# A layernorm, gated feed-forward and Fourier-mixing kernel: a different reciprocal root and order of products in the opening, and a unit's four row tiles of the down product in one place

## The chip, the cores and the metric

The kernel runs on one core of a Trainium2 chip. The metric is the device time of one execution in microseconds (us). The kernel before took 769.42, 769.16 and 769.20 us in three runs, a median of 769.2. Engines: TensorE (PE, with its weight loads as PEld), VectorE (DVE), ScalarE (ACT), GpSimd (POOL) and SyncE (SP), which issues DMAs.

## The reference

```python
xn = layernorm(x)                      # x: 2048 rows of 448, eps 1e-5
a, b = xn @ dft_hid_re.T, xn @ dft_hid_im.T
s = dft_seq_re @ a - dft_seq_im @ b    # 2048 x 2048 by 2048 x 448
g = (gelu_tanh(xn @ w_gate) * (xn @ w_up)) @ w_down   # 448 -> 1792 -> 448
out = x + s * silu(g)
```

All of it is float32.

## The kernel before

**Precision.** Products run in a float32 format of the matrix unit that takes fewer bits than float32. Each operand is therefore kept as a high part and a low part (what the high part leaves), and a product is three: high by high, high by low, low by high. In the first products these are called "h0" or "hh" (high by high), "hl", and "lh" or "l0" (the low part of the weight); "last" is the last block of the contraction, which needs fewer. A high part is a copy by ScalarE, a low part a subtraction by VectorE or GpSimd.

**Stages.** The 2048 rows are 16 tiles of 128 in four chunks `c`, tile `k` of chunk `c` being `xr[c][:, k]`. The hidden dimension of 1792 is 14 blocks `f` of 128, in seven pairs, `GROUPS`. An opening normalizes and transposes chunk after chunk, and does the gate and up products of the first pair; groups 1 to 6 do those of the other pairs and the down products; the Fourier mixing follows, for the last 370 us, and is not touched.

**The opening.** SyncE loads tiles 0 and 1, the two raw weight blocks (`load_w`, `f` = 0 in two halves) and the other tiles. `stats` normalizes: `one` takes mean and variance on VectorE (`one.s` on ScalarE), `root` the square root on ScalarE, `newton` the reciprocal and one Newton step on VectorE, `norm` scales the tile. `turn_mm` transposes a tile on TensorE into a PSUM bank `pt`; ScalarE copies it out as the high part and VectorE subtracts for the low part (`turn_split`, in the first two tiles written out). `prep_w` splits the first weights by `high`, `low` and `rest`. `first(f, cols, parts)` issues products of the first chunk, for a half of its columns. `warm(n)` is n products on zeros, whose result nothing reads, put in where TensorE would stand.

**A unit.** Groups 1 to 6 have four units `bi` = 0 to 3, each one `f` and a pair `p` of chunks, done in `strassen` as seven sums of products in place of eight: 39 products of 512 columns, by `three` (L473) and `two` (L480), into four PSUM banks x1 to x4, which every unit uses again in that order. In a unit's second half: x1 is gelu'd by ScalarE into `g1` (L521), VectorE adds x3 to `u` into `c21` (L525) and multiplies `g1` by it (L526), ScalarE copies the high part of the hidden block `hs` out (L528) and VectorE subtracts for its low part (L530); VectorE adds x4 to `u` (L534) and ScalarE gelus it (L535). The other chunk's hidden block is finished in the next unit by `late` (L539, L541, L544).

**The down products.** A row tile of the down product is six products of 448 columns (`down_one`, L450) into a bank `po`; ScalarE copies it out (L457), and behind the fourth row tile of a chunk GpSimd issues a DMA (L462) that adds the chunk to `gs` in DRAM. They are kept in a list `dq` and issued one by one by `send` at places `dn[0]` to `dn[3]` of each unit: behind x2, behind x4's first half, behind x3 and at the end. `preps[0]` to `preps[3]` are four places for the splitting of the next weights (`prep_s`, L356 to L362, and `prep_d`, L384 and L385).

**What sets the order.** The program is scheduled by hand: each engine runs its instructions in the order in which the code issues them, and waits on semaphores for the others. `sums_s` issues ten additions or subtractions of 128 columns on GpSimd (L338 to L347), which make the sums of the next group's raw weights; it is called at the start of units `bi` = 1 and 2 in groups 2 to 5. `sum_step`, behind a unit, issues other DMAs, those that accumulate on GpSimd (L809). So in GpSimd's queue stand, in this order, the DMA of the down product of the unit that ends, in some units two DMAs of `sum_step`, and the sums.

Of the kernel before, what the change touches and what calls it, by code (L numbers as in the profile page):

```python
# [45 lines left out]
def fnet_geglu(ctx: ExitStack, tc: tile.TileContext, x, ca, ct, cp, et, wgu, wd, out):  # L46
# [45 lines left out]
    def tmp(i):  # L92
        return a_t[:, 512 * i : 512 * i + 512]
# [55 lines left out]
    def stats(c, k0, n):  # L149
        st = const.tile([P, 4, 6], F32, name=f"st{c}_{k0}", tag="st", bufs=2)  # L150
        mv = const.tile([P, 4, 2], F32, name=f"mv{c}_{k0}", tag="mv", bufs=3)
        sd = const.tile([P, 4, 4], F32, name=f"sd{c}_{k0}", tag="sd", bufs=3)

        def one(i):
            nc.vector.bn_stats(st[:, i], xr[c][:, k0 + i, :D])
            nc.vector.bn_aggr(mv[:, i], st[:, i])

        def one_s(i):

            xi, (mean, var), q = xr[c][:, k0 + i, :D], [mv[:, i, e : e + 1] for e in (0, 1)], sd[:, i, 2:3]  # L160
            nc.scalar.activation(tmp(0)[:, :D], xi, AF.Identity, accum_out=q)
            nc.scalar.activation(mean, q, AF.Copy, scale=1.0 / D)
            nc.scalar.activation(sd[:, i, 3:4], q, AF.Copy, scale=-1.0 / D)
            nc.scalar.activation(tmp(0)[:, :D], xi, AF.Square, bias=sd[:, i, 3:4], accum_out=q)
            nc.scalar.activation(var, q, AF.Copy, scale=1.0 / D)

        one.s = one_s

        def root():
            r, t, w = sd[:, :n, 0], sd[:, :n, 1], sd[:, :n, 2]  # L170
            nc.scalar.activation(t, mv[:, :n, 1], AF.Sqrt, bias=epst)
            nc.vector.tensor_scalar(w, mv[:, :n, 1], EPS, -0.5, op0=ALU.add, op1=ALU.mult)
            nc.vector.tensor_scalar_mul(sd[:, :n, 3], mv[:, :n, 0], -1.0)

        def newton():
            r, t, w = sd[:, :n, 0], sd[:, :n, 1], sd[:, :n, 2]
            nc.vector.reciprocal(r, t)

            nc.vector.tensor_mul(t, r, r)
            nc.vector.tensor_mul(t, t, w)  # L180
            nc.vector.scalar_tensor_tensor(r, t, 1.5, r, op0=ALU.add, op1=ALU.mult)

        def norm(i, eng=nc.vector):
            v = xr[c][:, k0 + i]
            if eng is nc.scalar:
                eng.activation(v, v, AF.Identity, bias=sd[:, i, 3:4])
                eng.activation(v, v, AF.Copy, scale=sd[:, i, 0:1])
            else:
                eng.tensor_scalar(
                    v, v, mv[:, i, 0:1], sd[:, i, 0:1], op0=ALU.subtract, op1=ALU.mult  # L190
                )

        return one, root, newton, norm
# [288 lines left out]
    def strassen(f, p, w, late, dn, preps):  # L482
# [42 lines left out]
        nc.vector.tensor_add(c21, u, x3)  # L525
# [20 lines left out]
        return late0, late1  # L546

    units_n = [0]


    with tc.manual_schedule():
# [15 lines left out]
        nc.scalar.activation(tbl, epst, AF.Sqrt)  # L567


        def warm(n):  # L570
            t = o_tile(f"warm{n}")
            for _ in range(n):
                nc.tensor.matmul(t, junk[:, :P], junk, start=True, stop=True)  # L573
# [5 lines left out]
        def first(f, cols, parts, gs=range(2)):  # L579

            for part in parts:
                if part == "h0":
                    for n, k in enumerate((1, 2, 0)):
                        for g in gs:
                            nc.tensor.matmul(  # L585
                                pgs[f][g][:, cols], block(ws[f], k, g)[0], xk(0, k)[:, cols],
                                start=n == 0, stop=False, skip_group_check=True,
                            )
                    continue
                for g in gs:  # L590
# [32 lines left out]
        nc.scalar.activation(xh[1], t1[2], AF.Copy)  # L623
        nc.vector.tensor_sub(xl[0], t0[2], xh[0])
        high0(None, 0, 512)
        low0(nc.gpsimd, 256, 512)
        rest0(nc.gpsimd)
        one, root, newton, norm = stats(0, 2, 2)
        nc.vector.tensor_sub(xl[1], t1[2], xh[1])
        one(0)  # L630
        high1(None, 512)
# [19 lines left out]
        turn_split(t2, t3, mid=lambda: one.s(3), ahead=lambda: (one(1), one(2), root()))  # L651
# [6 lines left out]
        first(1, half[1], ("lh",), (0,))  # L658
        t0, t1 = turn_mm(1, 0), turn_mm(1, 1)
        first(1, half[1], ("lh",), (1,))  # L660
        first(1, half[1], ("last",))
# [153 lines left out]
        def send():  # L815
            if dq:
                down_one(*dq.pop(0))

        nop = lambda: None

        e_at, e_raw = {}, {}

        def e_load(b):
# [19 lines left out]
        for gi in range(1, len(GROUPS)):  # L843
# [7 lines left out]
            for bi, (i, p) in enumerate(zip((0, 1, 1, 0), sides)):  # L851
# [55 lines left out]
                else:  # L907
# [501 lines left out]
```

## Time and profile before

| | us |
|---|---|
| median of three runs | 769.2 |
| the profiled execution, device time | 769.27 |
| its span in the profile | 767.5 |
| TensorE busy | 761.3 (99%) |
| VectorE busy | 544.4 (71%) |
| ScalarE busy | 366.6 (48%) |
| GpSimd busy | 179.9 (23%) |
| mean granted TensorE clock | 0.999 |

The page is of one execution. Its busy times say how full an engine is over the whole span; the chain that ended last says on which engine's work the end depends. A row of the timeline gives the start in us from the span's start, the length, engine, line and operation, the tiles written and read, and, in brackets, how long the engine had been idle and what ended that. A row with "x6" is six instructions in a row, and its length reaches from the first start to the last end. A row of the chain of waits gives start, length and what ran.

### The profile page before, as it was taken

The numbers are of one execution on the slowest core, as the hardware profiler recorded it, in microseconds if no ns is written. First come the engines' busy times: TensorE is split into PE (matmuls) and PEld (weight loads), VectorE is DVE, ScalarE is ACT, GpSimd is POOL, SyncE is SP. The second block draws the span as 40 slices with busy tenths as digits, with TensorE's granted clock in tenths as the row PEclk, the third lists the DMA queues.
The fourth block names the chain that finished last, engine by engine and source line by source line (L and its number), as shares of the span: only waits on it lengthen the run. The fifth ranks groups of instructions, "written<-read, shape, count | busy, mean of one in ns | idle before, by whom it ended". The sixth has DMA issues, their size and how long they took to land.

```text
span 767.5 us, 11360 instructions
## 1 busy us (share of the span) xinstructions
PE 761.3 (99%) x4054; PEld 686.2 (89%) x4054; DVE 544.4 (71%) x946; ACT 366.6 (48%) x547; POOL 179.9 (23%) x303
## 2 busy tenths in 40 slices
PE   8999999999999999999999999999999999999998
PEld 7988888888888888888889999999999999999997
DVE  7879877555556556455452777978888797979787
ACT  5975554444444344344444585534444444434341
POOL 2204043430501511501011001223222222323130
PEclk9999999999999999999999999999999999999999
DMA  8234458994959968774979981959696969688794
GB/s 298 91 120 150 145 203 172 263 186 104 266 107 252 272 117 225 172 157 84 257 218 240 372 346 54 325 170 334 210 354 205 346 202 343 211 304 268 256 312 153
DMA packets 61513, 170.04 MB, mean 222 GB/s; under 512 B 7440, under 2 KB 40080, under 8 KB 60560
## 3 DMA queue, kind: packets, MB, share of 16 engines
q0 software_dynamic: 13728, 61.02, 35.0%
q1 hardware_dynamic: 34272, 82.48, 30.5%
q10 hardware_dynamic: 13456, 25.81, 9.2%
q8 instruction: 32, 0.52, 0.3%
q14 instruction: 25, 0.20, 0.1%
HBM read 127.21 MB, written 70.91 MB: 258 GB/s over the span
## 4 chain that ended last, share of the span: by engine, by line
PE 99%; DVE 0%; issue 0%; DVEq 0%
PE x L473 24%; PE p L1173 22%; PE po L450 18%; PE p L1176 10%; PE ab L984 9%; PE x L480 4%; PE gu L396 4%; PE py L1188 1%; PE py L1190 1%; PE py L1189 1%; PE gu L599 1%; PE pt L198 1%; PE warm L573 1%; PE p L1206 0%; PE gu L585 0%
## 5 line engine op out<-in xcount | busy, mean ns | idle before, releaser
L473 PE MATMUL x<-xt,w 128*128 128x512 f32 x480 | 149.6, 392 | 0.0
L473 PEld LDWEIGHTS x<-xt,w 128*128 128x128 f32 x480 | 90.1, 188 | 16.3 <-DVE tmp L512 0.7
L457 ACT ACTIVATE po_out<-po 128x448 f32<-128x448 f32 x112 | 60.2, 537 | 81.7 <-PE po L450 79.5
L450 PE MATMUL po<-wd0h,hs 128*128 128x448 f32 x256 | 81.7, 366 | 0.0
L462 POOL DMA_DIRECT2D gs<-po_out x24 | 21.4, 893 | 218.7 <-ACT po_out L457 213.7
L984 PE MATMUL ab<-e,xt 128*128 128x448 f32 x288 | 68.8, 365 | 0.0
L450 PE MATMUL po<-wd,hs 128*128 128x448 f32 x288 | 66.0, 365 | 0.0
L473 PE MATMUL x<-t_v,w 128*128 128x512 f32 x216 | 60.8, 390 | 0.0
L450 PEld LDWEIGHTS po<-wd,hs 128*128 128x128 f32 x288 | 54.1, 188 | 6.7
L984 PEld LDWEIGHTS ab<-e,xt 128*128 128x128 f32 x288 | 54.1, 188 | 4.3
L450 PEld LDWEIGHTS po<-wd0h,hs 128*128 128x128 f32 x256 | 48.1, 188 | 4.9
L473 PEld LDWEIGHTS x<-t_v,w 128*128 128x128 f32 x216 | 40.6, 188 | 8.7
L1064 POOL DMA_DIRECT2D raw<-sums x45 | 24.8, 552 | 94.9 <-DVE xt L143 56.6
L450 PE MATMUL po<-wd0l,hs 128*128 128x448 f32 x128 | 46.9, 367 | 0.0
L142 ACT ACTIVATE e<-raw 128x896 fp32r<-128x896 f32 (+1 forms) x30 | 27.6, 921 | 38.6 <-DVE raw L1071 27.8
L528 ACT ACTIVATE hs<-tmp 128x512 fp32r<-128x512 f32 x24 | 15.2, 634 | 54.6 <-DVE tmp L526 54.6
L473 PE MATMUL x<-t_lo,w 128*128 128x512 f32 x96 | 37.4, 389 | 0.0
L142 ACT ACTIVATE e<-tmp 128x896 fp32r<-128x896 f32 (+1 forms) x22 | 19.7, 896 | 35.7 <-DVE tmp L1071 28.6
L1173 PE MATMUL p<-t_v,wd0l 128*128 128x448 f32 x112 | 36.4, 374 | 0.0
L1173 PE MATMUL p<-w,e 128*128 128x448 f32 x112 | 36.4, 374 | 0.0
L1064 POOL DMA_DIRECT2D tmp<-sums x39 | 21.5, 552 | 59.9 <-DVE xt L143 37.2
L358 DVE TENSOR_TENSOR w<-raw,w 128x512 fp32r<-128x512 f32 (+1 forms) x24 | 21.3, 888 | 18.3 <-ACT w L356 18.3
(374 smaller groups left out, 2017.6 us busy)
## 6 DMA issues: line engine op xcount, KB each, us to landing
gs<-po_out POOLq DMA_DIRECT2D x24, 896.0 KB, 7.8
sums<-ca SPq DMA_DIRECT2D x16, 896.0 KB, 11.2
sums<-ca POOLq DMA_DIRECT2D x16, 896.0 KB, 14.5
t_v<-td ACTq DMA_DIRECT2D x24, 448.0 KB, 5.8
w<-td ACTq DMA_DIRECT2D x24, 448.0 KB, 7.5
raw<-ct SPq DMA_DIRECT2D x45, 192.0 KB, 4.2
raw<-wgu SPq DMA_DIRECT2D x12, 640.0 KB, 5.9
tmp<-ct SPq DMA_DIRECT2D x39, 192.0 KB, 4.6
```

The source lines that it names most:

```text
L142: nc.scalar.activation(h, src, AF.Copy)
L358: nc.vector.tensor_sub(w[:, 1408 + lo : 1408 + b], raw[:, P + lo : P + b], hw[:, lo:b].bitcast(F32))
L396: nc.tensor.matmul(ps[:, cols], a, xt[:, cols], start=n == 0, stop=n == len(mm) - 1)
L450: nc.tensor.matmul(po[:, :D], hs[:, a, kk * P : (kk + 1) * P], wdn[b][:, i], start=n == 0, stop=n == 5,)
L457: nc.scalar.activation(out_[0][:, kk], po[:, :D], AF.Copy)
L462: nc.gpsimd.dma_start(gv[:, 4 * c : 4 * c + 4], out_[0], accum_op=ALU.add)
L473: nc.tensor.matmul(ps, a[i], b[j], start=first and n == 0, stop=n == 2, skip_group_check=True)
L480: nc.tensor.matmul(ps, a[0], xt, start=False, stop=True, skip_group_check=True)
L984: nc.tensor.matmul(p[:, :D], a, b, start=n == 0, stop=n == len(mm) - 1)
L1064: nc.gpsimd.dma_start(v[:, 4 * P : 6 * P], sums[j][:, KS.index(k)])
L1173: nc.tensor.matmul(ps[q][:, :D], h, v, start=u % UN == 0, stop=False, skip_group_check=True)
L1176: nc.tensor.matmul(ps[q][:, :HD], l, v[:, :HD], start=False, stop=u % UN == NS - 1, skip_group_check=True,)
```

## The change

In the opening, `root` becomes one ScalarE function that gives the reciprocal root at once; `newton` keeps the Newton step, in two operations per tile for a statistic of two tiles. Both halves of a weight's high part are copied by ScalarE (one of them was a VectorE cast), the low parts of the second weight go from GpSimd to VectorE, the two halves of the first weight's load change places, one product of `warm` goes, and the products of the first half-chunk are put in another order: both weights' high-by-high and the first weight's low-by-high come first. In groups 2 to 6, 17 of the 20 units issue their four row tiles together at `dn[1]`, in the middle, and the second step of the weight splitting ahead of them; group 1 and the last three units of group 6 keep their places.

```diff
         def root():
-            nc.scalar.activation(t, mv[:, :n, 1], AF.Sqrt, bias=epst)
-            nc.vector.tensor_scalar(w, mv[:, :n, 1], EPS, -0.5, op0=ALU.add, op1=ALU.mult)
-            nc.vector.tensor_scalar_mul(sd[:, :n, 3], mv[:, :n, 0], -1.0)
+            nc.scalar.activation(sd[:, :n, 0], mv[:, :n, 1], AF.Abs_reciprocal_sqrt, bias=epst)
         def newton():
-            nc.vector.reciprocal(r, t)
+            nc.vector.tensor_scalar(w, mv[:, :n, 1], EPS, -0.5, op0=ALU.add, op1=ALU.mult)
+            if n == 2:
...
+                for i in range(2):
+                    nc.vector.scalar_tensor_tensor(
+                        ti[i], ri[i], wi[i], ri[i], op0=ALU.mult, op1=ALU.mult
+                    )
+                for i in range(2):
+                    nc.vector.scalar_tensor_tensor(
+                        ri[i], ti[i], 1.5, ri[i], op0=ALU.add, op1=ALU.mult
+                    )
+                return
...
-        for b in (4, 0) if f == 0 else (None,):
+        for b in (0, 4) if f == 0 else (None,):
...
-        warm(4)
+        warm(3)
...
-        high0(nc.vector.tensor_copy, 512)
+        high0(None, 0, 512)
+        high0(None, 512)
         low0(nc.gpsimd, 512)
+        low0(nc.gpsimd, 256, 512)
+        rest0(nc.gpsimd)
...
         high1(None, 512)
-        one(1)
+        high1(None, 0, 512)
         root()
-        high1(None, 0, 512)
-        low1(nc.gpsimd, 256, 512)
-        rest1(nc.gpsimd)
...
         low1(nc.vector, 512)
+        low1(nc.vector, 256, 512)
+        rest1(nc.vector)
...
-        first(0, half[0], ("h0", "hl", "lh", "last"))
-        first(1, half[0], ("h0", "hl"))
+        first(0, half[0], ("h0", "l0"))
+        first(1, half[0], ("h0",))
+        first(0, half[0], ("hl", "last"))
+        first(1, half[0], ("hl",))
         t2, t3 = turn_mm(0, 2), turn_mm(0, 3)
-        first(1, half[0], ("lh", "last"))
+        first(1, half[0], ("l0", "last"))
...
         preps[1]()
+        if dn[0] is nop:
+            preps[2]()
         dn[1]()
...
-        preps[2]()
+        if dn[0] is not nop:
+            preps[2]()
...
-                dn = [send] * 4
-                if gi == 1 and bi < 2:
-                    dn = [nop, send, nop, send]
+                dn = [nop, lambda: [send() for _ in range(4)], nop, nop]
+                if gi == 1 or (bi and not nxt):
+                    dn = [send] * 4 if gi > 1 or bi > 1 else [lambda: None, send, nop, send]
```

ScalarE's first instructions before, from the first root on (`sd` holds the statistics, `pt` a transposed tile, `raw_74` and `raw_75` the two raw weights):

```order
L171 ACTIVATE sd_0_124<-mv_0_123,epst 128x2
L622 ACTIVATE xt_66<-pt_0_137 128x4x128
L623 ACTIVATE xt_66<-pt_1_143 128x4x128
L314 ACTIVATE w<-raw_74 128x512
L314 ACTIVATE wd_78<-raw_75 128x512
L171 ACTIVATE sd_2_163<-mv_2_162,epst 128x2
L314 ACTIVATE wd_78<-raw_75 128x512
```

The same place now:

```order
L174 ACTIVATE sd_0_124<-mv_0_123,epst 128x2
L326 ACTIVATE w<-raw_74 128x512 x2
L641 ACTIVATE xt_66<-pt_0_136 128x4x128
L642 ACTIVATE xt_66<-pt_1_142 128x4x128
L326 ACTIVATE wd_78<-raw_75 128x512 x2
L174 ACTIVATE sd_2_160<-mv_2_159,epst 128x2
```

The weight copies of the first weight stand ahead of the transposed tiles, and both of the second ahead of the second root.

VectorE before, from the first root on (`xr_a` holds the tiles of rows that are scaled):

```order
L172 TENSOR_SCALAR sd_0_124<-mv_0_123 128x2
L173 TENSOR_SCALAR sd_0_124<-mv_0_123 128x2
L177 RECIPROCAL sd_0_124<-sd_0_124 128x2
L179 TENSOR_TENSOR sd_0_124<-sd_0_124 128x2
L180 TENSOR_TENSOR sd_0_124<-sd_0_124 128x2
L181 SCALAR_TENSOR_TENSOR sd_0_124<-sd_0_124 128x2
L189 TENSOR_SCALAR xr_a<-xr_a,mv_0_123,sd_0_124 128x512 x2
L316 CAST w<-raw_74 128x512
```

The same place now:

```order
L178 TENSOR_SCALAR sd_0_124<-mv_0_123 128x2
L182 SCALAR_TENSOR_TENSOR sd_0_124<-sd_0_124 128x1 x2
L186 SCALAR_TENSOR_TENSOR sd_0_124<-sd_0_124 128x1 x2
L201 TENSOR_SCALAR xr_a<-xr_a,mv_0_123,sd_0_124 128x512 x2
L644 TENSOR_TENSOR xt_66<-pt_0_136,xt_66 128x4x128
L645 TENSOR_TENSOR xt_66<-pt_1_142,xt_66 128x4x128
```

Four steps on both tiles at once have become two steps for each tile, and the cast of the first weight is gone.

TensorE in the first unit of group 2 (`f` = 4, `p` = 1; the banks are x1 = `x_4_1_1225`, x2 = `x_4_1_1235`, x3 = `x_4_1_1252`, x4 = `x_4_1_1260`; `po_2_k` is row tile k of chunk 2), before, from the end of x2 on:

```order
L450 MATMUL po_2_0_1244<-wd_78,hs_80 128x448 x3
L450 MATMUL po_2_0_1244<-wd_78,hs_79 128x448 x3
L473 MATMUL x_4_1_1252<-xt_69,w 128x512
L473 MATMUL x_4_1_1252<-t_lo,w 128x512
L473 MATMUL x_4_1_1252<-xt_69,w 128x512
L473 MATMUL x_4_1_1252<-t_v_822,w 128x512 x3
L473 MATMUL x_4_1_1260<-xt_69,w 128x512
L473 MATMUL x_4_1_1260<-t_lo,w 128x512
L473 MATMUL x_4_1_1260<-xt_69,w 128x512
L473 MATMUL x_4_1_1260<-t_v_822,w 128x512 x3
L450 MATMUL po_2_1_1271<-wd_78,hs_80 128x448 x3
L450 MATMUL po_2_1_1271<-wd_78,hs_79 128x448 x3
```

Now, from x4's first half on (x4 is `x_4_1_1246`):

```order
L485 MATMUL x_4_1_1246<-xt_69,w 128x512
L485 MATMUL x_4_1_1246<-t_lo,w 128x512
L485 MATMUL x_4_1_1246<-xt_69,w 128x512
L485 MATMUL x_4_1_1246<-t_v_816,w 128x512 x3
L462 MATMUL po_2_0_1259<-wd_78,hs_80 128x448 x3
L462 MATMUL po_2_0_1259<-wd_78,hs_79 128x448 x3
L462 MATMUL po_2_1_1267<-wd_78,hs_80 128x448 x3
L462 MATMUL po_2_1_1267<-wd_78,hs_79 128x448 x3
L462 MATMUL po_2_2_1275<-wd_78,hs_80 128x448 x3
L462 MATMUL po_2_2_1275<-wd_78,hs_79 128x448 x3
L462 MATMUL po_2_3_1283<-wd_78,hs_80 128x448 x3
L462 MATMUL po_2_3_1283<-wd_78,hs_79 128x448 x3
```

The first row tile has moved behind x3 and x4, the third and fourth ahead of the rest of x1 and x3, so that the 24 products of the four stand in a row.

ScalarE in the second unit of group 2 (`f` = 5, `p` = 1), before: L500 copies x1, L541 is of the unit ahead.

```order
L500 ACTIVATE tmp<-x_5_1_1332 128x512
L541 ACTIVATE hs_79<-tmp 128x512
L457 ACTIVATE po_out<-po_3_0_1351 128x448
L457 ACTIVATE po_out<-po_3_1_1375 128x448
L521 ACTIVATE tmp<-x_5_1_1332 128x512
L528 ACTIVATE hs_79<-tmp 128x512
L457 ACTIVATE po_out<-po_3_2_1397 128x448
L535 ACTIVATE tmp<-tmp 128x512
L457 ACTIVATE po_out<-po_3_3_1413 128x448
```

Now:

```order
L512 ACTIVATE tmp<-x_5_1_1326 128x512
L556 ACTIVATE hs_79<-tmp 128x512
L469 ACTIVATE po_out<-po_3_0_1361 128x448
L469 ACTIVATE po_out<-po_3_1_1369 128x448
L469 ACTIVATE po_out<-po_3_2_1377 128x448
L469 ACTIVATE po_out<-po_3_3_1385 128x448
L535 ACTIVATE tmp<-x_5_1_1326 128x512
L543 ACTIVATE hs_79<-tmp 128x512
L550 ACTIVATE tmp<-tmp 128x512
```

All four copies of row tiles stand ahead of the gelu of x1 (L521, now L535), and so the fourth, behind which GpSimd's DMA goes, does. On GpSimd no instruction of a unit has changed its place in the queue.

More of the change, by code (lines that the diff above doesn't have):

```diff
@@ L548, in fnet_geglu @@
     units_n = [0]
+    nop = lambda: None
     with tc.manual_schedule():
@@ L566, in fnet_geglu @@
         tbl = const.tile([P, 1], F32, name="tbl")
-        nc.scalar.activation(tbl, epst, AF.Sqrt)
+        nc.scalar.activation(tbl, epst, AF.Abs_reciprocal_sqrt)
         def warm(n):
@@ L581, in first @@
             for part in parts:
-                if part == "h0":
+                if part in ("h0", "l0"):
                     for n, k in enumerate((1, 2, 0)):
@@ L585, in first @@
                             nc.tensor.matmul(
-                                pgs[f][g][:, cols], block(ws[f], k, g)[0], xk(0, k)[:, cols],
-                                start=n == 0, stop=False, skip_group_check=True,
+                                pgs[f][g][:, cols], block(ws[f], k, g)[part == "l0"], xk(0, k)[:, cols],
+                                start=part == "h0" and n == 0, stop=False, skip_group_check=True,
                             )
@@ L619, in fnet_geglu @@
         (high0, low0, rest0, _), (high1, low1, rest1, _) = ws
-        high0(nc.vector.tensor_copy, 512)
+        high0(None, 0, 512)
+        high0(None, 512)
         low0(nc.gpsimd, 512)
+        low0(nc.gpsimd, 256, 512)
+        rest0(nc.gpsimd)
         nc.scalar.activation(xh[0], t0[2], AF.Copy)
         nc.scalar.activation(xh[1], t1[2], AF.Copy)
+        one, root, newton, norm = stats(0, 2, 2)
         nc.vector.tensor_sub(xl[0], t0[2], xh[0])
[L625 to L628, printed above, removed]
         nc.vector.tensor_sub(xl[1], t1[2], xh[1])
         one(0)
+        one(1)
         high1(None, 512)
-        one(1)
+        high1(None, 0, 512)
         root()
-        high1(None, 0, 512)
-        low1(nc.gpsimd, 256, 512)
-        rest1(nc.gpsimd)
         for k, t in enumerate((t0, t1)):
@@ L642, in fnet_geglu @@
         low1(nc.vector, 512)
+        low1(nc.vector, 256, 512)
+        rest1(nc.vector)
         ws = [w[3] for w in ws]
         draw = load_d(GROUPS[0], a_r[0][:, 1024:])
-        first(0, half[0], ("h0", "hl", "lh", "last"))
-        first(1, half[0], ("h0", "hl"))
+        first(0, half[0], ("h0", "l0"))
+        first(1, half[0], ("h0",))
+        first(0, half[0], ("hl", "last"))
+        first(1, half[0], ("hl",))
         t2, t3 = turn_mm(0, 2), turn_mm(0, 3)
-        first(1, half[0], ("lh", "last"))
+        first(1, half[0], ("l0", "last"))
         one, root, newton, norm = stats(1, 0, 4)
         one(0)
-        turn_split(t2, t3, mid=lambda: one.s(3), ahead=lambda: (one(1), one(2), root()))
+        var3 = one.s(3)
+        one(1)
+        turn_split(t2, t3, mid=var3, ahead=lambda: (one(2), root()))
         newton()
@@ L657, in fnet_geglu @@
         first(1, half[1], ("hh", "hl"))
-        first(1, half[1], ("lh",), (0,))
         t0, t1 = turn_mm(1, 0), turn_mm(1, 1)
-        first(1, half[1], ("lh",), (1,))
-        first(1, half[1], ("last",))
+        first(1, half[1], ("lh", "last"))
         turn_split(t0, t1)
@@ L817, in send @@
                 down_one(*dq.pop(0))
-        nop = lambda: None
         e_at, e_raw = {}, {}
```

9 lines of the change are left out of this document (6 added, 3 removed).

## The prediction

> **What bounds the kernel now.** I read the page first, then the waits by engine, then the chain of waits in order of time, and last the timeline of the opening and of single units.
>
> The page's first and fourth parts, and the waits of TensorE:
>
> ```profile
> PE 761.3 (99%) x4054; PEld 686.2 (89%) x4054; DVE 544.4 (71%) x946; ACT 366.6 (48%) x547; POOL 179.9 (23%) x303
> PE 99%; DVE 0%; issue 0%; DVEq 0%
> PE warm L573 <- DVE hs L563: 1.5, 1, 1.5
> PE pt L198 <- issue: 0.8, 1, 0.8
> ```
>
> TensorE is busy for 99% of the span and is itself 99% of the chain. It waits only in the opening, so every other engine matters only through the slack that it has before TensorE needs its result. A change can gain by shortening the opening or by making products closer; it can lose by using up slack.
>
> The chain of waits in order of time, with start, length and number of products; the last four rows are one whole unit, with its middle left out, and the first product of the next:
>
> ```profile
> 14.72 5.66 PE gu L599 x47
> 20.38 0.87 PE pt L198 x8
> ...
> 61.91 4.86 PE po L450 x24
> 71.78 5.44 PE x L473 x24
> 122.36 2.74 PE x L473 x12
> 125.10 1.21 PE po L450 x6
> 126.32 2.74 PE x L473 x12
> ...
> 136.14 0.46 PE x L473 x2
> ```
>
> A unit has 39 products of 512 columns and four row tiles of six products of 448; it takes 136.14 - 122.36 = 13.78 us without a gap.
>
> **The change, part by part.**
>
> *Opening.* The timeline of before, start and length first:
>
> ```profile
> 5.24 0.30 ACT L171 ACTIVATE sd<-mv,epst 128x2 f32<-128x2 f32 x1 [2.99 <-DVE mv L156]
> 5.57 0.17 DVE L177 RECIPROCAL sd<-sd 128x2 f32<-128x2 f32 x1
> ...
> 6.16 0.16 DVE L181 SCALAR_TENSOR_TENSOR sd<-sd 128x2 f32<-128x2 f32 x1
> 6.36 1.00 DVE L189 TENSOR_SCALAR xr_a<-xr_a,mv,sd 128x512 f32<-128x512 f32 x2
> 7.01 1.07 PE L198 MATMUL pt<-ident,xr_a 128*128 128x128 f32 x8 [0.76 <-issue]
> ...
> 8.84 0.99 PE L585 MATMUL gu<-xt,w 128*128 128x256 f32 x6
> ...
> 9.74 0.63 ACT L314 ACTIVATE wd<-raw 128x512 fp32r<-128x512 f32 x1 [0.47 <-DMA raw<-wgu]
> ...
> 12.23 1.72 DVE L189 TENSOR_SCALAR xr_a<-xr_a,mv,sd 128x512 f32<-128x512 f32 x2
> ...
> 13.34 1.39 PE L198 MATMUL pt<-ident,xr_a 128*128 128x128 f32 x8
> 15.78 0.88 PE L599 MATMUL gu<-xt,w 128*128 128x256 f32 x6
> ```
>
> The first normalization begins when four dependent VectorE steps are through, 5.57 to 6.36, 0.20 us each. The new root gives the reciprocal at once and newton is two dependent steps, so the normalization starts at 5.97 and everything behind it, to the first gate product, 0.39 us earlier (8.45). ScalarE's new function is not in the trace; between 0.17 us (a VectorE step on the same 128x2) and 0.63 (ScalarE over 512 columns) I take the 0.30 of the root, the same engine on the same tile. An error there is swallowed by the next step.
>
> This 0.39 does not last. Twelve products of f=0 now come first; at 0.12 us each (47 in 5.66) they end at about 9.9. The next ones need the high half of the second weight, whose copy starts at 9.74, behind the landing of its DMA, and takes 0.63: 10.45 with the hand-over. TensorE stands for 0.5 us. The 22 products that are then left ahead of the next transposes end at 10.45 + 22 x 0.12 = 13.1, where they end before too: the next transposes' wait begins there.
>
> The gain comes one step later. Before, the transposes of tiles 2 and 3 wait for normalizations that run at 12.23 in 1.72 us, where two took 1.00 at 6.36: they lie beside the low halves that GpSimd computes. The transposes start 0.2 late, at 13.34, and take 1.39 with a second wait in their middle, where eight take 0.87 at 20.38. The change ends the chain of statistics earlier and puts these low halves on VectorE behind the normalizations. Without these waits the transposes run from 13.1 to 14.0, ten products follow, and the first product of the second half starts at about 15.2 instead of 15.78. I take **-0.6 us**. The ends: 0.0 if the low halves of tiles 2 and 3, which I get ready at 16.5 for use at 16.65, come late; and -0.8 if the second copy of the high half hides better than I think.
>
> *Units, on TensorE.* 39 products cost 39 x 5.44/24 = 8.84 us in a row, plus 0.02 where the width changes (2.74 for twelve that follow a row tile, 2.72 for twelve in the long row), plus 4.86 for 24 products of row tiles: 13.72 instead of 13.78. Three switches fewer in each of 17 units: 17 x 0.055 = **-0.9 us**. The four row tiles have a bank each, so that block waits for no copy. The low half of the second weight step, now ahead of L525, has the 1.55 us for which VectorE idles ahead of it below as cover, and 4.9 us of row tiles more. SyncE's queue of loads is untouched.
>
> *Units, on GpSimd and VectorE.* No instruction is added here, but one moves. With the fourth row tile goes its copy and the accumulating DMA that GpSimd issues behind it; behind that DMA, in the same queue, stand the ten sums of the next group's weights. The timeline of the third unit of group 3, which starts at 204.84:
>
> ```profile
> 205.51 0.53 ACT L457 ACTIVATE po_out<-po 128x448 f32<-128x448 f32 x1
> 206.44 0.90 POOL L462 DMA_DIRECT2D gs<-po_out  x1 [5.44 <-ACT po_out L457]
> 207.07 0.77 POOL L338 TENSOR_TENSOR raw<-raw 128x128 f32<-128x128 f32 x1
> 208.46 2.84 DVE L544 TENSOR_TENSOR hs<-tmp,hs 128x512 fp32r<-128x512 f32 x1
> ...
> 210.01 0.72 POOL L345 TENSOR_TENSOR raw<-raw 128x128 f32<-128x128 f32 x1
> 210.81 0.80 POOL L346 TENSOR_TENSOR raw<-raw 128x128 f32<-128x128 f32 x1
> 211.69 0.46 POOL L347 TENSOR_TENSOR raw<-raw 128x128 f32<-128x128 f32 x1
> 215.23 0.69 DVE L525 TENSOR_TENSOR tmp<-tmp,x 128x512 f32<-128x512 f32 x1 [1.55 <-PE x L480]
> 216.03 0.69 DVE L526 TENSOR_TENSOR tmp<-tmp 128x512 f32<-128x512 f32 x1
> 216.75 0.64 ACT L528 ACTIVATE hs<-tmp 128x512 fp32r<-128x512 f32 x1 [2.05 <-DVE tmp L526]
> 217.42 0.69 DVE L530 TENSOR_TENSOR hs<-tmp,hs 128x512 fp32r<-128x512 f32 x1 [0.70 <-ACT hs L528]
> 218.03 0.68 DVE L534 TENSOR_TENSOR tmp<-tmp,x 128x512 f32<-128x512 f32 x1
> ```
>
> L544 has both inputs in SBUF. Its like at L530 takes 0.69 us; begun 1.39 us behind L338, it takes 2.84, and ends at 211.30, L338 + 4.23, in the pause between L345 and L346. L525, one input in PSUM, is not slowed in this manner. So while GpSimd runs its sums back to back, a VectorE operation on two SBUF inputs stands until they pause. In before this hits L544, which nobody needs soon.
>
> Now the clock of the changed unit, counted from its end E. The row tiles follow 24 products, from 5.46 to 10.32 after its start; ScalarE begins to copy the last one some 0.18 behind its piece and takes 0.53, to 11.03, E - 2.69. The DMA starts 0.40 behind that (206.44 against 206.04) and L338 0.63 behind the DMA: E - 1.66. The products of x3 end five products before E, E - 1.13; L525 follows 0.19 later, E - 0.94 (in before they end 10.20 after the unit's start, 215.04, and L525 stands at 215.23), and L526 0.80 later, E - 0.14. That is L338 + 1.52, in the middle of the run of sums. If it stands as L544 did, it ends at E + 2.57; L528 then runs to E + 3.24, L530 to about E + 4.0 and L534, which empties the bank of x4, to E + 4.6. The next unit writes this bank with its nineteenth product, at E + 18 x 0.227 = 4.08. TensorE waits 0.55 to 0.65 us, and loses 0.11 on the product behind a wait, as here (0.33 between starts instead of 0.23):
>
> ```profile
> 103.44 0.50 PE L473 MATMUL x<-xt,w 128*128 128x512 f32 x1
> 103.77 0.39 PE L473 MATMUL x<-t_lo,w 128*128 128x512 f32 x1
> ```
>
> That makes 0.7. The sums stand at the start of the second and third units of groups 2 to 5, so eight boundaries are hit. At three of them two more DMAs stand ahead of the sums:
>
> ```profile
> 151.89 2.03 POOL L809 DMA_DIRECT2D sums<-ca  x2
> 153.00 1.41 POOL L338 TENSOR_TENSOR raw<-raw 128x128 f32<-128x128 f32 x1
> 153.36 0.69 DVE L544 TENSOR_TENSOR hs<-tmp,hs 128x512 fp32r<-128x512 f32 x1
> 154.48 0.75 POOL L340 TENSOR_TENSOR raw<-raw 128x128 f32<-128x128 f32 x1
> ```
>
> There L338 comes some 1.1 later, E - 0.59, and L340 1.48 behind it instead of 0.84. L544, 0.36 behind L338, got through in 0.69. L526 at L338 + 0.45 should too; but L530, due at E + 1.2, then meets the run, stands until about E + 3.6, and L534 ends at about E + 4.9: 1.0 with the 0.11. In all 5 x 0.7 + 3 x 1.0 = **+6.5 us**. The lower end is 0, if no operation stands; the upper, with half as much again at each, is 9.
>
> The sum on the profiled run: 769.27 (a span of 767.5 and 1.77 around it) - 0.6 - 0.9 + 6.5 = 774.3; the median shown is 0.07 lower, so **774.2 us**.
>
> The Trainium skill, page "SBUF — State Buffer", section "SBUF: two separate sides", calls the port pair that VectorE and GpSimd share an exclusive lock, which whoever starts first holds "for the whole instruction"; it concerns VectorE operations with two SBUF inputs against a GpSimd operation that reads SBUF. By it L526 would stand for what is left of one sum. The trace agrees that there is a lock, but its 2.84 us reach over five sums, so it is handed over only where GpSimd pauses; I go by the trace.
>
> **The rivals.**
>
> *No boundary waits* (the other side). If the lock is passed after each sum, L526 loses the 0.4 us between two sums (L338 to L345 are 2.94 us for seven), and L530 and L534 as much; L534 ends at E + 2.5 without any of it, and has 1.5 us before it matters. Then only the two gains are left: 769.2 - 1.5 = 767.7, at the edge of what counts as faster. It holds as long as all delays on this way stay under 1.5 us. For it: the sums are ten instructions, and between any two of them there is a place to hand over; that at 153.36 got through. Against it: the 2.84 above. Here the page's rule gives 767.7 as well.
>
> *Only the five plain boundaries wait.* If L530 slips between sums at the other three, as L544 did at 153.36, the loss is 3.5: 771.2. For it: their sums start late and unevenly. Against: L340 on, they run as evenly as elsewhere.
>
> *Longer waits.* If GpSimd's last sums (L346, L347, up to L338 + 5.1) hold up L530 or L534 as well, or the opening's gain falls away, 776 to 778. For it: L347 lies at E + 3.0 to 3.4, where L530 wants to start. Against: L516 at 212.00, one SBUF input, was not held there.
>
> **How the numbers follow.** Eight boundaries, 774.2 (own range 772.7 to 775.9): 0.53. Five, 771.2: 0.18. None, 767.7: 0.15, about half of it beyond 0.2% faster. Longer, 776 to 778: 0.10. Some other part of the eight, 769 to 770: 0.04. A measurement of this kernel tells about 0.2%, 1.5 us, from no change. Faster 0.08, same 0.09, slower 0.83. The range leaves out the case with no waits and the upper half of the long ones: 770.0 to 777.0.
>
> **What would show it.** In the profile after: the waits of TensorE name x4's first product behind the VectorE addition to u, about eight times, 0.5 to 1 us each; the multiplication of g1 by c21 (0.69 alone) takes some 2.7 us at five boundaries; a unit away from them takes 13.72; the first product of the second half stands at 15.2. If the multiplication takes 0.7 everywhere while the sums run, the step about the port is wrong, and the time is near 767.7.

## The result and the profile after

| | before | after |
|---|---|---|
| median device time, us | 769.31 | 775.75 |
| profiled execution, us | 769.27 | 775.97 |
| its span, us | 767.5 | 774.2 |
| start of the first unit of group 1 | 71.62 | 71.61 |
| start of the last unit of group 6 | 383.89 | 390.22 |

The changed kernel is slower: ratio 1.0084, 95% interval 1.0073 to 1.0095. All of the difference but 0.4 us lies between the two starts in the table, 318.61 us instead of 312.27, so in the units; the opening gives nothing. One of the six executions of the kernel before took 1112.59 us; the median of the other five is 769.20.

The page of after, its first and fourth parts, and the waits of TensorE:

```profile
PE 762.3 (98%) x4053; PEld 685.3 (89%) x4053; DVE 555.4 (72%) x942; ACT 371.9 (48%) x548; POOL 178.1 (23%) x301
PE 92%; DVE 5%; DMA 1%; ACT 1%; SPq 0%; issue 0%; DVEq 0%
PE x L485 <- DVE tmp L549: 4.8, 8, 1.0
PE warm L589 <- DVE hs L579: 1.5, 1, 1.5
PE gu L601 <- ACT xt L642: 0.6, 1, 0.6
PE gu L601 <- ACT wd L326: 0.5, 1, 0.5
```

VectorE has come onto the chain, with 5%, and is busy for 11 us more although it executes four instructions fewer: it is being held, not working. TensorE waits eight times for the addition to `u`, now L549. The last two rows are new waits in the opening.

Where VectorE's 11 us are, from the groups by line between 122 and 350 us (count, busy time, mean ns of one, then idle time ahead): the multiplication, which took 0.69 us each, and the low half.

```profile
L541 DVE TENSOR_TENSOR tmp<-tmp 128x512 f32<-128x512 f32 x16 | 21.9, 1370 | 1.7
L545 DVE TENSOR_TENSOR hs<-tmp,hs 128x512 fp32r<-128x512 f32 x16 | 18.3, 1141 | 11.2 <-ACT hs L543 11.2
L540 DVE TENSOR_TENSOR tmp<-tmp,x 128x512 f32<-128x512 f32 x16 | 11.0, 688 | 64.0 <-PE x L492 64.0
```

16 x (1.370 - 0.69) is 10.9 us, and 16 x (1.141 - 0.69) is 7.2; L540, which reads one of its inputs from PSUM, takes what it always took. (L544 before, hit by the same in the first half of a unit, 0.96 us on average, has become quick, so VectorE's total grows by less.)

The timeline at the end of the second unit of group 3 (in before, sums began 2.2 us behind this place, and held L544); the next unit starts at 207.63:

```profile
205.38 0.90 POOL L474 DMA_DIRECT2D gs<-po_out  x1 [7.32 <-ACT po_out L469]
206.01 0.77 POOL L350 TENSOR_TENSOR raw<-raw 128x128 f32<-128x128 f32 x1
206.70 0.69 DVE L540 TENSOR_TENSOR tmp<-tmp,x 128x512 f32<-128x512 f32 x1 [4.71 <-PE x L492]
207.49 2.74 DVE L541 TENSOR_TENSOR tmp<-tmp 128x512 f32<-128x512 f32 x1
208.96 0.71 POOL L357 TENSOR_TENSOR raw<-raw 128x128 f32<-128x128 f32 x1
209.75 0.80 POOL L358 TENSOR_TENSOR raw<-raw 128x128 f32<-128x128 f32 x1
210.93 0.71 DVE L545 TENSOR_TENSOR hs<-tmp,hs 128x512 fp32r<-128x512 f32 x1 [0.70 <-ACT hs L543]
211.56 0.68 DVE L549 TENSOR_TENSOR tmp<-tmp,x 128x512 f32<-128x512 f32 x1
212.29 0.50 PE L485 MATMUL x<-xt,w 128*128 128x512 f32 x1 [0.42 <-DVE tmp L549]
```

GpSimd's DMA (L474) and its sums (L350 on) have come ahead of the unit's end. L541 stands from 207.49 until the run L350 to L357 is through, and ends at 210.23. The next unit's nineteenth product, due at 207.63 + 4.08 = 211.71, starts at 212.29.

The same at a boundary with two more DMAs ahead of the sums; the next unit starts at 192.62:

```profile
191.48 1.46 POOL L827 DMA_DIRECT2D sums<-ca  x1
192.04 1.73 POOL L350 TENSOR_TENSOR raw<-raw 128x128 f32<-128x128 f32 x1
192.48 0.99 DVE L541 TENSOR_TENSOR tmp<-tmp 128x512 f32<-128x512 f32 x1
193.85 0.74 POOL L352 TENSOR_TENSOR raw<-raw 128x128 f32<-128x128 f32 x1
194.16 3.05 DVE L545 TENSOR_TENSOR hs<-tmp,hs 128x512 fp32r<-128x512 f32 x1 [0.70 <-ACT hs L543]
195.94 0.72 POOL L357 TENSOR_TENSOR raw<-raw 128x128 f32<-128x128 f32 x1
197.14 0.67 DVE L549 TENSOR_TENSOR tmp<-tmp,x 128x512 f32<-128x512 f32 x1
197.87 0.50 PE L485 MATMUL x<-xt,w 128*128 128x512 f32 x1 [1.01 <-DVE tmp L549]
```

Here the multiplication gets in ahead of the run, and the low half behind it takes the full hold, 3.05 us.

The chain of waits in a unit that no wait touches, the last of group 2:

```profile
165.31 5.44 PE x L485 x24
170.75 4.87 PE po L462 x24
175.62 0.70 PE x L485 x3
...
179.05 0.45 PE x L485 x2
```

Such a unit takes 13.73 us from start to start, instead of 13.77.

The opening, from the timeline up to 17 us:

```profile
5.95 1.00 DVE L201 TENSOR_SCALAR xr_a<-xr_a,mv,sd 128x512 f32<-128x512 f32 x2
7.25 0.63 ACT L326 ACTIVATE w<-raw 128x512 fp32r<-128x512 f32 x1 [1.16 <-DMA raw<-wgu]
7.79 0.58 ACT L641 ACTIVATE xt<-pt 128x512 fp32r<-128x512 f32 x1
8.91 1.69 PE L601 MATMUL gu<-xt,w 128*128 128x256 f32 x12 [0.55 <-ACT xt L642]
10.37 1.15 ACT L326 ACTIVATE wd<-raw 128x512 fp32r<-128x512 f32 x2 [1.52 <-DMA raw<-wgu]
11.05 1.03 PE L601 MATMUL gu<-xt,wd 128*128 128x256 f32 x6 [0.46 <-ACT wd L326]
13.84 1.03 PE L210 MATMUL pt<-ident,xr_a 128*128 128x128 f32 x8
15.91 1.36 PE L615 MATMUL gu<-xt,w 128*128 128x256 f32 x10
```

The normalization starts at 5.95, 0.41 earlier than before, and there the gain ends: ScalarE holds the copy of the transposed tile behind a copy of the weight's second half, which waits for its DMA until 7.25, so the first product starts at 8.91 (8.84 before). Then TensorE waits for the second weight, whose landing stands at 10.35 here. The second half begins at 15.91, not at 15.2.

### The profile page after: what moved, and what is told of

The parts are those of the page before. It is cut to its first block, busy times and chain, and to the rows that moved or that the text cites. A ratio compares the mean times of both kernels' runs of the same rounds, so it can differ in the third digit from the quotient of the medians.

```text
span 774.2 us, 11361 instructions
## 1 busy us (share of the span) xinstructions
PE 762.3 (98%) x4053; PEld 685.3 (89%) x4053; DVE 555.4 (72%) x942; ACT 371.9 (48%) x548; POOL 178.1 (23%) x301
## 4 chain that ended last, share of the span: by engine, by line
PE 92%; DVE 5%; DMA 1%; ACT 1%; SPq 0%; issue 0%; DVEq 0%
PE p L1190 21%; PE x L485 19%; PE po L462 18%; PE p L1193 10%; PE ab L1001 9%; PE gu L408 4%; PE x L492 4%; DVE tmp L541 2%; DVE hs L545 2%; PE py L1205 1%; PE py L1207 1%; PE py L1206 1%; PE gu L615 1%; DMA raw<-wgu 1%; PE pt L210 1%; DVE tmp L540 1%
## 5 line engine op out<-in xcount | busy, mean ns | idle before, releaser
L462 PE MATMUL po<-wd0h,hs 128*128 128x448 f32 x256 | 78.0, 367 | 0.0
L474 POOL DMA_DIRECT2D gs<-po_out x24 | 21.4, 893 | 225.3 <-ACT po_out L469 225.2
L540 DVE TENSOR_TENSOR tmp<-tmp,x 128x512 f32<-128x512 f32 x24 | 16.5, 687 | 73.0 <-PE x L492 73.0
L462 PE MATMUL po<-wd,hs 128*128 128x448 f32 x288 | 61.8, 365 | 0.0
L543 ACT ACTIVATE hs<-tmp 128x512 fp32r<-128x512 f32 x24 | 15.2, 633 | 61.6 <-DVE tmp L541 61.6
L545 DVE TENSOR_TENSOR hs<-tmp,hs 128x512 fp32r<-128x512 f32 x24 | 25.4, 1057 | 16.8 <-ACT hs L543 16.8
```

Source lines behind the costliest of these rows:

```text
L462: nc.tensor.matmul(po[:, :D], hs[:, a, kk * P : (kk + 1) * P], wdn[b][:, i], start=n == 0, stop=n == 5,)
L545: nc.vector.tensor_sub(hs[:, 1], g1, hs[:, 0])
```

## The experiments

Each was timed against the kernel before on the same chip. The units from group 2 on and the opening were first taken apart.

**The opening alone**: the changed kernel with the old places of the row tiles.

```diff
-                dn = [nop, lambda: [send() for _ in range(4)], nop, nop]
...
+                dn = [send] * 4
+                if gi == 1 and bi < 2:
+                    dn = [lambda: None, send, nop, send]
```

> The changed opening with the units of before. Theory (the opening gives nothing: ScalarE's first transposed copy stands behind a weight copy that waits for its DMA, and the second weight's landing sets the next products): 769.3, within 0.2 of before. Rival, the opening saves 0.6 us as predicted and the changed kernel's profile caught a late landing: 768.7. Both expect the first product of the first unit at 71.6 us or up to 0.6 earlier, and no wait in the units.

Measured: 769.72 us against 769.18, ratio 1.0005 (0.9996 to 1.0014). In its profile the first unit starts at 71.95, 0.33 later than before; from the last product to the end it takes 0.36 us more (4.38 for 4.02, counted from that product's start). The opening saves nothing; if anything it costs.

**The units alone**: the kernel before with only `dn` and the place of `preps[2]` changed.

> The opening of before with the changed units. Theory (all of the loss lies in the units): 775.7, that is before + 6.4, and eight waits of TensorE behind the VectorE addition to u, 4 to 5 us in all. Rival, the opening has a part in it (the changed opening shifts the DMAs of later stages): 775.1 or less.

Measured: 775.49 against 769.18, ratio 1.0085 (1.0072 to 1.0099), and the same eight waits for the addition, 4.8 us in all, longest 1.0. The loss is in the units. The 0.26 us that it lies below the changed kernel's 775.75 are found behind the last product: 4.39 us in the changed kernel's profile, 4.04 in this one.

**The sums later**: only GpSimd's sums leave the unit's end; the DMA ahead of them stays.

```diff
+        if gated:
+            nc.gpsimd.tensor_copy(gate_t, late[0].hs[:, 1, :1].bitcast(F32))
+            gated.pop(0)()
         preps[0]()
...
-                            sums_s(n_raw[0], nc.gpsimd)
+                            gated.append(lambda r=n_raw[0]: sums_s(r, nc.gpsimd))
```

> The changed kernel, but GpSimd's ten sums start behind a one-column GpSimd copy that reads the hidden block's low half of the same unit (some 3.5 us into the unit), so the DMA behind the fourth row tile stays where it is and only the sums leave the unit's end. Theory (the sums hold up VectorE's operations on two SBUF inputs): no wait at x4, multiplication 0.7 us everywhere, units of 13.73, 768.6. Rival, the DMA of the row tiles or the traffic behind it holds VectorE up: the waits stay, 775 to 776. Rival, the end of a unit is simply too tight once the row tiles are gone from it: the waits shrink only in part, 771 to 774.

Measured: 769.01 (ratio 0.9997, 0.9988 to 1.0005), no wait in the units, each 13.73. The groups by line of VectorE:

```profile
L544 DVE TENSOR_TENSOR tmp<-tmp 128x512 f32<-128x512 f32 x16 | 11.1, 693 | 1.7
L548 DVE TENSOR_TENSOR hs<-tmp,hs 128x512 fp32r<-128x512 f32 x17 | 11.8, 692 | 11.9 <-ACT hs L546 11.9
```

Multiplication (here L544) and low half are back at 0.69. The DMA of the row tiles is where the change put it, so neither it nor the tight end of the unit is the cause: the sums are. The time is 0.4 above the expected 768.6; in this profile the first unit starts 0.18 late (71.80) and 0.36 us more pass behind the last product (4.38), and the run of the old opening below has neither (71.58, 4.02).

**The product in PSUM**: the sums stay beside the unit's end, but VectorE no longer has two SBUF inputs there.

```diff
-        nc.vector.tensor_add(c21, u, x3)
-        nc.vector.tensor_mul(g1, g1, c21)
+        nc.vector.tensor_add(x3 if dn[0] is nop else c21, u, x3)
+        pr = x3 if dn[0] is nop else g1
+        nc.vector.tensor_mul(pr, g1, x3 if dn[0] is nop else c21)
...
-        nc.vector.tensor_sub(hs[:, 1], g1, hs[:, 0])
+        nc.vector.tensor_sub(hs[:, 1], pr, hs[:, 0])
```

> The changed kernel with the sums where they are, but c21 and its product with g1 are written to x3's PSUM bank, so that the multiplication and the subtraction for the low half have one SBUF input each. Theory (only operations with two SBUF inputs are held): neither waits although the sums run beside them, no wait at x4, 768.6. Rival, GpSimd's run slows VectorE whatever its inputs: the multiplication still takes over 2 us and the time stays at 774 to 776.

Measured: 768.85 (ratio 0.9997, 0.9988 to 1.0006), no wait in the units. The timeline at the same boundary; this unit's successor starts at 204.00:

```profile
202.35 0.77 POOL L350 TENSOR_TENSOR raw<-raw 128x128 f32<-128x128 f32 x1
203.87 0.70 DVE L542 TENSOR_TENSOR x<-tmp,x 128x512 f32<-128x512 f32 x1
204.45 0.72 POOL L355 TENSOR_TENSOR raw<-raw 128x128 f32<-128x128 f32 x1
205.23 0.69 DVE L546 TENSOR_TENSOR hs<-x,hs 128x512 fp32r<-128x512 f32 x1 [0.67 <-ACT hs L544]
205.29 0.71 POOL L357 TENSOR_TENSOR raw<-raw 128x128 f32<-128x128 f32 x1
```

The multiplication (L542) comes 1.52 us behind L350, nearly at the phase of the run (1.48) at which it took 2.74 in the changed kernel, and takes 0.70; so does the low half. Its result goes to PSUM here too, but that is not what frees it: L540 of the changed kernel, with one input in PSUM, writes to SBUF and took 0.69 beside the sums (206.70). In the units GpSimd does not slow VectorE as such; it holds the operations that need a second SBUF input.

**The sums in another order**: same work, same place, but with sums that read the one before next to each other.

```diff
         eng.tensor_sub(s3, g0, u0)
+        eng.tensor_sub(u2d, g2d, u2d)
+        eng.tensor_add(u2d, u2d, g3)
+        eng.tensor_sub(u2d, u2d, u3)
+        eng.tensor_add(u0, u0, u1)
+        eng.tensor_sub(s2, u0, g0)
+        eng.tensor_sub(s4, g1, s2)
         eng.tensor_sub(s7, g2, u2)
...
```

> The changed kernel with the ten sums in another order: the three that build on each other (u2d) second to fourth, then u0, s2, s4, each of which reads the one before, so that GpSimd pauses between most of them instead of ahead of the last two alone. Theory (VectorE gets the port in the first pause of GpSimd's run): the multiplication takes 0.7 to 1.3 us at the plain boundaries, no wait at x4 there, 768.6 to 770. Rival, the port stays with GpSimd until its queue of sums is empty: the multiplication still takes 2.5 us or more, 775 to 777.

Measured: 768.73 against 769.23 (ratio 0.9994, 0.9985 to 1.0003), no wait in the units. The timeline at this boundary; the next unit starts at 204.68:

```profile
203.46 0.75 POOL L351 TENSOR_TENSOR raw<-raw 128x128 f32<-128x128 f32 x1
204.29 0.46 POOL L352 TENSOR_TENSOR raw<-raw 128x128 f32<-128x128 f32 x1
204.54 0.76 DVE L541 TENSOR_TENSOR tmp<-tmp 128x512 f32<-128x512 f32 x1
204.83 0.79 POOL L353 TENSOR_TENSOR raw<-raw 128x128 f32<-128x128 f32 x1
205.58 0.46 POOL L354 TENSOR_TENSOR raw<-raw 128x128 f32<-128x128 f32 x1
```

A sum that reads the one before starts 0.08 us after that one has ended (L351 ends at 204.21, L352 starts at 204.29; L352 ends at 204.75, L353 starts at 204.83), where the sums of the changed kernel start 0.42 us apart and overlap. In the pause behind L352 L541 gets in, and takes 0.76. L353 behind it takes 0.79, not the 0.46 of L352, so now GpSimd stands. Ten sums still run beside the unit's end. What held VectorE was that nothing parted them.

**The old opening with the changed units and the product in PSUM.**

> The opening of before, and the changed units with c21 and the product in x3's bank. Theory (the units alone are worth 17 x 0.04 = 0.7 once nothing waits, and the changed opening costs some 0.3 on average): 768.5. Rival, the changed opening is worth what its best profile shows, 0.45: this kernel is then slower than the same with the changed opening, 768.85, at about 769.0.

Measured: 768.52 against 769.23, ratio 0.9992 (0.9983 to 1.0001). The moved row tiles are worth 0.7 us when nothing waits, a little under the 0.9 predicted. The interval of the time just includes no change, but the profile shows it: units of 13.73 instead of 13.77.

**The opening taken apart.** All four that follow have the product in PSUM, so that the units do not wait. First, the products of the first half in the old order:

```diff
-        first(0, half[0], ("h0", "l0"))
-        first(1, half[0], ("h0",))
-        first(0, half[0], ("hl", "last"))
-        first(1, half[0], ("hl",))
+        first(0, half[0], ("h0", "hl", "lh", "last"))
+        first(1, half[0], ("h0", "hl"))
```

> The product in x3's bank, and the changed opening but with the order of products of before (all of f=0 first, then f=1). Theory (the order of products makes TensorE meet the second weight's landing at 9.4 to 10.4 us; in the old order it is first read some 2.7 us after the first product): no wait behind the second weight's copy, the first unit at 71.2 to 71.5 in every run, 768.2 to 768.6. Rival, the late first product (8.7 to 9.5, behind the first weight's second landing) is the larger part: first unit at 71.6 or later, 768.8 or more.

Measured: 768.75 (ratio 0.9995, 0.9986 to 1.0003), the first unit at 71.42. The wait behind the second weight is gone; the late first product (8.93) and a wait of 0.3 us for the low halves of tiles 2 and 3 remain. The time is above the 768.2 to 768.6 expected, and against 768.85 with the new order no difference can be told.

Second, the copies of the transposed tiles ahead of the first weight's second half (and the two loads of that weight in the order of before, outside the lines shown):

```diff
-        high0(None, 0, 512)
         high0(None, 512)
-        low0(nc.gpsimd, 512)
...
         nc.scalar.activation(xh[1], t1[2], AF.Copy)
+        high0(None, 0, 512)
+        low0(nc.gpsimd, 512)
```

> The product in x3's bank, and the changed opening with the halves of the first weight loaded in the order of before and ScalarE's copies of the transposed tiles ahead of the second half's copy. Theory (ScalarE's queue holds the transposed copies behind a weight copy that waits for its DMA): the first product at about 8.5 instead of 8.7 to 9.5, and TensorE then waits for the second weight instead, 0.5 to 1.2; the first unit's start depends on that landing as before, 768.5 to 769.0. Rival, the late landings are of the swapped load order: then the second weight lands at 9.4 to 9.7 and the time is 768.2.

Measured: 768.62 (ratio 0.9991, 0.9982 to 1.0000), but the first product only at 9.43. The expectation missed what its profile shows:

```profile
6.03 2.00 DVE L201 TENSOR_SCALAR xr_a<-xr_a,mv,sd 128x512 f32<-128x512 f32 x2
6.48 1.27 POOL L331 TENSOR_TENSOR w<-raw,w 128x512 fp32r<-128x512 f32 x1 [5.15 <-ACT w L326]
8.09 0.66 PE L210 MATMUL pt<-ident,xr_a 128*128 128x128 f32 x4 [0.78 <-DVE xr_a L201]
```

With the weight's first half copied sooner, GpSimd's subtraction starts at 6.48, while the first normalization runs, and the second is done only at 8.03: two take 2.00 us instead of 1.00, so a normalization is held by GpSimd too. Of ScalarE's queue, which the run was to show, it shows nothing: the first product waits for this normalization. The second weight landed at 10.39 with the old order of loads, so a late landing does not need the swapped halves.

Third and fourth, all of it mended: old order of products and of the first weight's loads, copies first, GpSimd's subtraction behind the second normalization, one tile's statistics behind the low halves that were late; then also the second root between the second weight's copies.

```diff
+        nc.gpsimd.tensor_copy(gate_t, xr[0][:, 1, :1])
         low0(nc.gpsimd, 512)
...
-        one(1)
-        turn_split(t2, t3, mid=var3, ahead=lambda: (one(2), root()))
+        turn_split(t2, t3, mid=var3, ahead=lambda: (one(1), one(2), root()))
```

> The product in x3's bank; in the opening the new root, the transposed copies ahead of the first weight's second half on ScalarE, the products of the first half in the order of before, the statistics of one later tile behind the low halves of tiles 2 and 3 on VectorE, and GpSimd's first subtraction of low parts behind a one-column copy that reads the second normalized tile (in the run with the copies first, that subtraction held the second normalization for 1 us). Theory (three things ate the opening's gain: ScalarE's queue behind a late DMA, the product order that meets the second weight's landing, and the port held by GpSimd during a normalization): first product at 8.4 to 8.6, first unit at 70.9 to 71.2 whatever the landings, 767.8 to 768.2. Rival, the landings of the first weight set the first product anyway: first product at 8.8 or later and 768.5 or more.

> The same, with the second root on ScalarE between the two copies of the second weight instead of behind both. Theory (the normalizations of tiles 2 and 3 are late behind the root, which stands behind the weight copies): the transposes of tiles 2 and 3 come up to 0.5 us earlier if they waited for them in the run above, and the time is 0 to 0.3 lower; no difference if they waited for TensorE alone.

Measured: 768.22 (ratio 0.9985, 0.9976 to 0.9995) and 767.89 (ratio 0.9983, 0.9974 to 0.9992), against 769.24. These two are the only ones whose interval lies wholly below no change. The first units start at 71.32 and 71.02, the first products at 8.95 and 8.64, so the 0.3 us between the profiles are there at the first product. Both miss the expected 8.4 to 8.6: the second because its normalization starts at 6.19, not at 5.95, and the first not for the rival's reason, the landing (6.49, against 5.79 in the second), as its rows show:

```profile
6.51 0.63 ACT L326 ACTIVATE w<-raw 128x512 fp32r<-128x512 f32 x1 [1.05 <-DMA raw<-wgu]
6.79 1.43 PE L210 MATMUL pt<-ident,xr_a 128*128 128x128 f32 x8
7.82 0.60 ACT L639 ACTIVATE xt<-pt 128x512 fp32r<-128x512 f32 x1 [0.67 <-PE pt L210]
```

The weight's copy is through at 7.14, and ScalarE then idles for the transposes of the first tiles. These take 1.43 us for eight, 1.07 in the second run: the products of `warm` just ahead of them start 0.43 us apart, in the second run 0.24 apart from 5.51 on. Why TensorE quickened later in that execution is not shown. The profile of the second:

```profile
8.64 1.02 PE L603 MATMUL gu<-xt,w 128*128 128x256 f32 x6
12.93 1.04 PE L210 MATMUL pt<-ident,xr_a 128*128 128x128 f32 x8
15.02 2.20 PE L617 MATMUL gu<-xt,w 128*128 128x256 f32 x17
```

Here are the opening's 0.6 us: the second half begins at 15.02 (15.78 before). Between the two kernels the intervals overlap, and the transposes of tiles 2 and 3 waited for TensorE in both (they start 0.72 behind the start of the last six products), so the earlier root itself is not shown to matter. This is the lowest median of all, 1.35 us under before.

## Why the prediction was right, and where its terms were off

| term, us | predicted | in the profile after |
|---|---|---|
| opening | -0.6 | 0.0 (71.61 for 71.62) |
| 17 units, closer products | -0.9 | -0.7 (17 x 0.04) |
| waits at five plain boundaries | +3.5 | +3.3 (0.59 to 0.71 each) |
| waits at three with DMAs ahead | +3.0 | +3.8 (1.24, 1.28, 1.30) |
| group 1 (units of 14.03 and 13.87 for 14.07 and 13.92) | 0 | -0.1 |
| behind the last product | 0 | +0.4 |
| sum | +5.0 | +6.7 |

A wait here is what its unit takes beyond the 13.73 us of a plain one. The sum is that of the spans, 774.2 - 767.5. The larger misses (the opening, the three boundaries, the time behind the last product) all go the same way, so the time lies above the forecast, inside the range; only the small ones, 0.1 to 0.2 us, cancel.

**The mechanism at the plain boundaries was right** in each of its steps. At the boundary shown, counted from the next unit's start at 207.63: L350 at -1.62 (predicted -1.66), L541 at -0.14 (-0.14), its end at +2.60 (+2.57), the end of L549 at +4.61 (+4.6). Three runs bear out the cause, by taking the sums from there, the second SBUF input from VectorE, or the lack of pauses from the sums; each alone removes all eight waits. The rival that no boundary waits had the lock passed after each sum: the run with the sums reordered shows that VectorE does get in between two sums, but only where the second one waits for the first. The rival of five waiting boundaries fell: at all eight TensorE waited. Of the rival of longer waits one half came, the loss of the opening's gain; the other did not: behind the held operation, L545 at the plain boundaries took 0.70 to 0.71, and L549 0.67 to 0.68 everywhere. One reading in the prediction does not carry what it is used for: L525 at 215.23, called not slowed, ran when the sums were over. L505 shows it, 0.69 at 207.85 in that same unit of before, with one input in PSUM and the sums beside it.

**At the three boundaries with DMAs ahead** the price was mis-sized, 1.0 for 1.27. The step said that L530 (now L545) stands until E + 3.6 and ends 0.7 later; at 192.62 it ended at E + 4.59. The multiplication ahead took 0.99 and held GpSimd in turn, so the run of sums began later than in the unit of before that it was read from: L352 stands 1.81 us behind L350, where L340 stood 1.48 behind L338.

**The opening** failed. The step was "so the normalization starts at 5.97 and everything behind it, to the first gate product, 0.39 us earlier (8.45)". The first half held (5.95). But the change also moves a weight copy ahead of the transposed copies in ScalarE's queue, and that copy waits for its DMA, until 7.25; the prediction put it at nothing, neither its 0.63 us nor its wait. And the landing of the second weight, behind which its copy starts at 9.74, was read from one execution; in six profiles with the changed opening the second half of the first weight landed at 6.8 to 7.8 us and the second weight at 9.4 to 10.4, and the new order of products needs both early. Where the second weight landed at 9.44, in the run with the product in PSUM, the first unit did start 0.45 earlier (71.16). The low end of the term, 0.0, was reached, but not for the reason given there: in the profile after nothing waits for the low halves of tiles 2 and 3. The opening of before reads that weight 2.8 us behind its first product, and starts its first unit within 0.04 us in three profiles (71.58 to 71.62).

**Units**: three changes of width fewer are worth 0.04 us, not 0.055. A unit of before takes 13.77 us (13.78 in the prediction), and 13.73 came where 13.72 was forecast.

**Left open**: why the weights landed later, on average, with the changed opening; and the 0.3 to 0.4 us behind the last product, in GpSimd's part of the closing barrier. Six profiles show them (4.38 to 4.46 us from the last product's start to the end), all with the changed opening's loads and copies of the first weight. The other six, with before's order of these loads (the three with the opening of before and the last three runs), show 4.02 to 4.04, one of these with the 301 GpSimd instructions of the changed kernel. So they go with that part of the opening; how it reaches the end is not shown.

## What to carry to other kernels

When work is moved along one engine's queue, ask what stands behind it in the queues that it releases: here a DMA that left 2.3 us before the unit's end pulled ten small sums with it, into the only place where VectorE's chain had no slack to spare. An operation on VectorE with two SBUF inputs stood for as long as GpSimd's run of sums was unbroken: put the run elsewhere, part it by dependences, or leave one of the inputs in PSUM. And an order that needs a load at the earliest time at which it was seen to land turns the spread of that time into the kernel's own.

## What the runs showed of the hardware

VectorE's operation with two SBUF inputs is not held for one GpSimd instruction but for a whole run that has no gap: 2.62 to 3.05 us at the eight boundaries, over the five or six sums that were under way or still to come. These overlap: each is shown 0.71 to 0.77 us long, and the next starts 0.42 behind it. Between two sums of which the second reads the first, and so starts 0.08 us after its end, the operation gets in (0.76). With one of two inputs in PSUM the same operation takes 0.69 to 0.70 in the middle of the run. The Trainium skill, page "SBUF — State Buffer", section "SBUF: two separate sides", has VectorE and GpSimd share a pair of ports that is held "for the whole instruction"; these runs agree that operations with two SBUF inputs are held and that those with one input in PSUM are not, and show a hold over several instructions.

A normalization (one SBUF tensor and two scalars per row) beside GpSimd's subtraction is held as well: two took 2.00 us instead of 1.00, so a second SBUF tensor is not the only way to be held.
